# A fused attention-and-MLP block on one core: 128-key V tiles, Q weights ahead of the second token pair, activation tables loaded ahead of use

## The chip, the core and the metric

The kernel runs on one core of a Trainium2 chip. A core has five engines that run their own instruction streams and wait for each other through semaphores: TensorE (PE, matmuls; its weight loads are listed apart as PEld), VectorE (DVE), ScalarE (ACT), GpSimd (POOL) and SyncE (SP, which here only issues DMAs). The metric is the device time of one execution in microseconds (us). Lower is better.

## The reference

Input x has 2048 tokens of width D = 448, all in bf16. Two blocks follow each other.

```
h   = x + A(layernorm(x))            # attention
out = h + B(layernorm(h))            # mixer and MLP

A: qkv = x @ wqkv  (16 heads of 28); each token attends to 8 keys: itself and
   the tokens 2, 4, ... 14 before it; softmax; concat; @ wo
B: h  = gelu(layernorm(x) @ w1)
   h is cut into 4 column groups, shifted along the tokens by +1, -1, +2, -2
   x1 = x + shifted @ w2
   x1 + gelu(layernorm(x1) @ w3) @ w4          # w3: 448 x 1792, w4: 1792 x 448
```

## The kernel before

**Layout.** A partition holds two neighbouring tokens (a = 0, 1: even and odd), and a "pair" m = 0..7 is a block of 128 partitions, 256 tokens. Since a query attends only to tokens of its own parity, even and odd tokens are two separate sequences of 1024. `xin` holds x and later h, `xb` the second residual. `HT` holds the normalised activations transposed: its upper 64 partitions belong to even tokens, the lower 64 to odd ones, in KB = 7 slices of 64 columns of D. A weight matrix is laid out to match: `wload` loads it in two halves, each half of the partitions starting with a different slice (`slot`), and two small transfers fill the slice left over. A matmul over 64 partitions for even tokens and one for odd tokens run in PE at the same time (planner mode "r64").

**Phases.** `phase_LN1(m)` takes statistics on DVE, the inverse root on POOL (`inv_std`: `vtmp`, `rstd`), two normalisations on DVE into `ln`, and a transpose into HT by `ln_to_HT`: on PE with a copy out of PSUM for pairs 0 and 1 (PET = 2), by a DMA transpose on SP's queue for the others. `phase_QK(u, nu)` projects Q (w = 0) and K (w = 1) for 256 x nu tokens per parity, from weights that `wqk_copies` spreads from `wst` (in `h3`) to 32 columns a head (`wqk_p`, in `arena`). `phase_V(t)` makes V for tile t. A tile t of the attention holds 114 queries of each parity in two halves h of NQ = 57, each half with its own 64 keys, which lie on its own 64 partitions. `phase_att(g)` does, for four tiles and one group of four heads, the scores (28x64 matmuls), Exp on ACT, a 0/1 mask on DVE (`msk`), row sums Z by matmuls with a column of ones, Ln and Exp of these on ACT (`lnz`), P·V (64x32 matmuls) and the product with 1/Z on DVE. `phase_WO`, `phase_LN2`, `phase_W1` (with GELU), `phase_W2`, `phase_LN3`, `phase_W3` (with GELU) and `phase_W4` follow. GELU and Exp/Ln need different activation tables, and `emit` puts an ACT_TABLE_LOAD ahead of an operation whose table isn't the loaded one (line 1356).

**Order.** The functions only list operations. `_Sched.schedule` (lines 233 to 377) then orders them, as a list planner with modelled durations: again and again, each engine names the operation that could start first, and among those within SLACK (100 ns) the one of the lowest rank in a list of phase names near the end of `_fast_path`. "flex" operations go to the engine where they would end first. The planner also hands out the 8 PSUM banks. `emit` writes each engine's stream in that order (all operations have line 1360, waits that stand alone line 1358). WARM = 36 matmuls on zeros ("warm") have a low rank.

**End.** `phase_flag` looks for non-finite statistics. Every engine waits for the flag, loads it (line 1398) and branches (1399) over `_general_path`, a full fallback program that doesn't run with these inputs. SP then waits for the outputs (1370), and all engines meet at line 1392.

Of the kernel before, what the change touches and what calls it, by code (L numbers as in the profile page):

```python
# [6 lines left out]
ALU = mybir.AluOpType  # L7
# [8 lines left out]
class _Op:  # L16
    __slots__ = ("idx", "eng", "ins", "kw", "dur", "deps", "users", "sem", "val", "t0", "t1", "clock", "is_dma",
                 "chan", "lat", "bulk", "odeps", "tag", "opts", "table", "prio", "groups", "mode", "xb")

    def __init__(self, idx, eng, ins, dur):  # L20
# [4 lines left out]
        self.is_dma = False; self.bulk = False; self.chan = None; self.lat = 0.0; self.odeps = set()  # L25
# [61 lines left out]
class _Sched:  # L87
# [88 lines left out]
    SWITCH = 300.0  # L176
    LEAD = -300.0
# [4 lines left out]
    def prepare(self):  # L182
        n = len(self.ops)
        for op in self.ops:
            for g in op.groups:
                if g.ops[0] is op:
                    own = set(g.ops)
                    for o in g.ops:
                        if o.eng == "pe":
                            op.odeps |= {d for d in o.deps if d not in own and d.idx < op.idx}  # L190
# [11 lines left out]
    def gated(self, ham, st, work):  # L202
# [3 lines left out]
        while work > 0.0:  # L206
# [7 lines left out]
            ham[1] += step  # L214
# [18 lines left out]
    def schedule(self):  # L233
# [5 lines left out]
        npend = list(self.npend)  # L239
        holder = [None] * 8  # L240
# [46 lines left out]
        table = None  # L287
        mode = None
# [4 lines left out]
        while done < n:  # L293
            best = None
            for e in engs:
                cand = None
                for op in ready[e]:
# [3 lines left out]
                    if cand is not None and st > cand[0] + self.SLACK:  # L301
# [16 lines left out]
                    if e == "act" and op.table is not None and op.table != table:  # L318
                        st = max(st, free[e] + self.TABLE) + self.SWITCH
                    if cand is None or st < cand[0] - self.SLACK or (st < cand[0] + self.SLACK and op.prio < cand[1].prio):  # L320
                        cand = (st, op)
                if cand is not None and (best is None or cand[0] < best[0]):
                    best = cand + (e,)
# [8 lines left out]
            if e == "act" and op.table is not None:  # L332
                if op.table != table:
                    st -= self.SWITCH
                table = op.table
            if e == "pe":
# [3 lines left out]
                dur = self.gated(ham, st, dur)  # L340
# [97 lines left out]
def _fast_path(nc, es, flag, A_x, A_wqkv, A_wo, B_w1, B_w2, B_w3, B_w4, out):  # L438
# [17 lines left out]
    wst = H3[:, 0:KB * 2 * D].rearrange("p (b n) -> p b n", b=KB)  # L456
    wv_s = sb("wv_s", [128, KB, D], BF16)
# [3 lines left out]
    NV = 6  # L461
    WARM = 36
    PET = 2
    NP = 3
    vt = sb("vt", [128, NV, 2, 16, 32], BF16)
    pt = sb("pt", [128, NP, 4, 8 * NQ], BF16)
    lnz = sb("lnz", [128, 2, 2, 8 * NQ], F32)
    lnup = sb("lnup", [128, 1], F32)
    msk = sb("msk", [128, 2, 8 * NQ], BF16)
# [11 lines left out]
    rstd = sb("rstd", [128, 4, 16], F32)  # L481
    vtmp = sb("vtmp", [128, 4, 16], F32)
# [19 lines left out]
    def copy(out_ap, in_ap, n):  # L502
# [3 lines left out]
            "dve": ([("tensor_copy", ka)], (150 + n) / 0.96)}, **ka)  # L506

    last = []

    def dma(chan, out_ap, in_ap, nbytes, dur=450.0, rate=200.0, q="sp", after=(), bulk=False):  # L510
        op = S.macro(q, [("dma_start", dict(out=out_ap, in_=in_ap))], dur, chan=chan, lat=(1200.0, nbytes / rate, 1150.0),
                     after=tuple(after) + tuple(last) if bulk else after, bulk=bulk)
        if bulk:
            last[:] = [op]
        return op
# [19 lines left out]
    def wload(chan, dst, src, qs, after=(), bulk=False, each=False):  # L535
        n = src.shape[1]
        for o in range(2):
            rows = src[64 * o:64 * o + 384, :].rearrange("(i p) n -> p i n", p=128)
            for i in range(3 if each else 1):
                i0, i1 = (i, i + 1) if each else (0, 3)  # L540
                dma(chan + qs[o], dst[:, 2 * i0 + o:2 * i1 + o - 1:2, :], rows[:, i0:i1, :], 128 * n * 2 * (i1 - i0), 500,
                    rate=300.0, q=qs[o], after=after, bulk=bulk)
        for a in range(2):
            dma(chan + qs[a], dst[half[a], 6, :], src[384:448, :] if a == 0 else src[0:64, :], 64 * n * 2, 500, rate=100.0, q=qs[a],
                after=after, bulk=bulk)

    uniq = [0]

    def ch(name):
        uniq[0] += 1  # L550
        return "%s_%d" % (name, uniq[0])

    def load_x(m, q="sp", after=()):
        dma("x%d" % m, xin[:, 2 * m:2 * m + 2, :].rearrange("p a n -> p (a n)"), xrows(A_x, m), 128 * D * 4, rate=333.0, q=q,
            after=after)

    def setup():
        S.tag = "setup"
        load_x(0)
        load_x(1)  # L560
        for w in range(2):
# [872 lines left out]
```

## Time and profile before

| what | value |
|---|---|
| median of 4 runs | 200.5 us (200.3 to 200.95) |
| profiled execution | 201.07 us |
| its span, first to last instruction | 199.3 us |
| PE / PEld / DVE / ACT / POOL busy | 188.6 / 123.3 / 111.1 / 99.2 / 48.3 us |
| instructions | 7192, of these 3279 matmuls and as many weight loads |
| DMA | 18.05 MB, mean 91 GB/s; 312 and 319 GB/s between 5 and 15 us |
| DMA transposes | 22, 3.1 us from issue to landing |
| landings, median | x 5.4 us, Q and K weights 4.4, outputs 1.9 |

A group line gives line, engine, operation, output<-input by the program's names, shape and count, then busy us and mean ns of one, then the idle time just ahead of it and what ended it. "issue" is time in which the engine waited for nothing that the profile shows. PE's matmuls overlap, so the mean ns of one is longer than their spacing; a spacing is found by dividing a group's busy time by its count. In the windows the numbers are the length, the busy time of PE, PEld, DVE, ACT and POOL with the count of instructions, the granted clock, the DMA share and GB/s.

### The profile page before, as it was taken

The numbers are of one execution on the slowest core, as the hardware profiler recorded it, in microseconds if no ns is written. First come the engines' busy times: TensorE is split into PE (matmuls) and PEld (weight loads), VectorE is DVE, ScalarE is ACT, GpSimd is POOL, SyncE is SP. The second block draws the span as 40 slices with busy tenths as digits, with TensorE's granted clock in tenths as the row PEclk, the third lists the DMA queues.
The fourth block names the chain that finished last, engine by engine and source line by source line (L and its number), as shares of the span: only waits on it lengthen the run. The fifth ranks groups of instructions, "written<-read, shape, count | busy, mean of one in ns | idle before, by whom it ended". The sixth has DMA issues, their size and how long they took to land.

```text
span 199.3 us, 7192 instructions
## 1 busy us (share of the span) xinstructions
PE 188.6 (95%) x3279; PEld 123.3 (62%) x3279; DVE 111.1 (56%) x262; ACT 99.2 (50%) x106; POOL 48.3 (24%) x90
## 2 busy tenths in 40 slices
PE   7899999899999999899899999999999999999980
PEld 2377765345455955569767555888875548855540
DVE  6987942653899449999979995100005830012220
ACT  2357689799397998539642400466660004620000
POOL 6313310000045001376330988000000370000000
PEclk9999999999999999999999999999999999999998
DMA  5998692414366333356883617200000160001111
GB/s 171 312 319 145 95 118 63 141 30 129 93 136 121 81 94 102 92 118 96 144 118 104 144 27 167 67 0 3 3 3 0 46 140 3 3 3 44 46 46 56
DMA packets 31515, 18.05 MB, mean 91 GB/s; under 512 B 21368, under 2 KB 31480, under 8 KB 31480
## 3 DMA queue, kind: packets, MB, share of 16 engines
q1 hardware_dynamic: 31480, 17.55, 38.8%
q8 instruction: 26, 0.43, 1.0%
q14 instruction: 9, 0.07, 0.2%
HBM read 10.67 MB, written 1.84 MB: 63 GB/s over the span
## 4 chain that ended last, share of the span: by engine, by line
PE 72%; DVE 11%; ACT 7%; DMA 4%; issue 1%; SPq 1%; POOL 1%
PE ps L1360 72%; DMA h<-in_A_wqkv_dram 3%; ACT QK L1360 2%; DVE xin L1360 2%; DVE QK L1360 2%; ACT lnz L1360 2%; DMA HT<-ln 2%; ACT pt L1360 2%; DVE ln L1360 2%; DVE xb L1360 2%; DVE st L1360 1%; DVE pt L1360 1%; ACT L1356 1%; SPq L1360 1%; POOL rstd L1360 1%
## 5 line engine op out<-in xcount | busy, mean ns | idle before, releaser
L1360 PE MATMUL ps<-HT,w_s 64*128 64x256 bf16 (+1 forms) x1064 | 56.1, 264 | 0.7 <-DMA HT<-ln 0.7
L1360 PEld LDWEIGHTS ps<-HT,w_s 64*128 64x128 bf16 x1064 | 50.5, 94 | 6.5 <-issue 1.1
L1360 DVE TENSOR_TENSOR xb<-ps,xb 128x448 bf16<-128x448 f32 (+1 forms) x24 | 18.6, 773 | 57.0 <-PE ps L1360 57.0
L1360 ACT ACTIVATE arena<-ps 128x1024 bf16<-128x1024 f32 x14 | 14.3, 1024 | 37.8 <-PE ps L1360 37.8
L1360 POOL TENSOR_SCALAR vtmp<-mv 128x2 f32<-128x2 f32 x32 | 6.2, 194 | 111.2 <-DVE mv L1360 109.8
L1360 ACT ACTIVATE QK<-ps 128x1024 bf16<-128x1024 f32 (+2 forms) x24 | 22.5, 952 | 15.3 <-PE ps L1360 15.2
L1360 PE MATMUL ps<-HT,arena 64*128 64x256 bf16 (+1 forms) x336 | 26.4, 305 | 1.0 <-issue 0.9
L1360 POOL TENSOR_TENSOR rstd<-vtmp,mhalf 128x2 f32<-128x2 f32 x32 | 22.1, 691 | 2.7
L1360 PE MATMUL ps<-w_s,arena 128*128 128x448 bf16 x112 | 21.7, 353 | 0.0
L1360 PE MATMUL ps<-w_s,h 128*128 128x448 bf16 x112 | 21.7, 353 | 0.0
L1360 PEld LDWEIGHTS ps<-HT,arena 64*128 64x128 bf16 x336 | 15.6, 94 | 9.6 <-issue 2.2
L1360 DVE BATCH_NORM_STATS2 st<-xin 128x6 f32<-128x448 bf16 x32 | 18.5, 612 | 0.4 <-DMA xin<-in_A_x_dram 0.3
L1360 PEld LDWEIGHTS ps<-w_s,h 128*128 128x128 bf16 x112 | 10.9, 98 | 10.3 <-issue 0.2
L1360 PEld LDWEIGHTS ps<-w_s,arena 128*128 128x128 bf16 x112 | 10.9, 98 | 10.2
L1360 ACT ACTIVATE h<-ps 128x1024 bf16<-128x1024 f32 x14 | 14.2, 1024 | 5.6 <-PE ps L1360 5.5
L1360 POOL TENSOR_TENSOR xb<-xb,xin 128x448 bf16<-128x448 bf16 x16 | 16.6, 1069 | 0.3 <-DVE ln L1360 0.3
L1360 DVE TENSOR_SCALAR ln<-xin,mv,rstd 128x448 bf16<-128x448 bf16 x32 | 14.6, 497 | 2.5 <-POOL rstd L1360 2.5
L1360 ACT ACTIVATE pt<-ps 128x912 bf16<-128x912 f32 x18 | 15.6, 932 | 0.3 <-PE ps L1360 0.2
L1360 DVE TENSOR_TENSOR QK<-ps,lnz 128x456 bf16<-128x456 f32 (+1 forms) x24 | 10.9, 509 | 8.0 <-ACT lnz L1360 4.3
L1360 DVE TENSOR_TENSOR pt<-pt,msk 128x912 bf16<-128x912 bf16 x18 | 11.2, 630 | 6.6 <-ACT pt L1360 5.0
L1360 PE MATMUL ps<-pt 128*128 128x512 bf16 x36 | 11.9, 469 | 1.4 <-DVE HT L1360 1.4
L1360 PE MATMUL ps<-w_s,QK 112*128 112x448 bf16 x64 | 13.0, 353 | 0.0
(53 smaller groups left out, 164.0 us busy)
## 6 DMA issues: line engine op xcount, KB each, us to landing
w_s<-in_B_w_dram SPq DMA_DIRECT2D x19, 224.0 KB, 2.6
xin<-in_A_x_dram SPq DMA_DIRECT2D x8, 224.0 KB, 5.4
out_dram<-xb SPq DMA_DIRECT2D x8, 224.0 KB, 1.9
h<-in_A_wqkv_dram SPq DMA_DIRECT2D x4, 336.0 KB, 4.4
wv_s<-in_A_wqkv_dram SPq DMA_DIRECT2D x2, 336.0 KB, 5.3
w_s<-in_B_w_dram SPq DMA_DIRECT2D x2, 336.0 KB, 3.0
w_s<-in_B_w_dram SPq DMA_DIRECT2D x4, 112.0 KB, 2.6
wo_s<-in_A_wo_dram SPq DMA_DIRECT2D x4, 98.0 KB
```

The costliest lines, as they stand in the source:

```text
L1356: eng.preload_act_table_set(_TABLE_SETS[table])
L1360: inst = getattr(eng, meth)(**kw)
```

## The change

The diff below is cut to its core. What it does, in the order of the code:

- **Planner**: a phase may have a head start (`ahead`, in ns, as `op.bonus`) in the choice among candidates; a PE operation that would run ahead of the modelled instruction fetch is put back; attention matmuls count 0.4 in the modelled clock gate; all ranks are new, and attention is ranked in two parts (attS, attP). When ACT has a modelled gap of 1.2 us or more, the next table is loaded at that gap (`op.load`).
- **Loads**: pair 0 of x comes in two halves, one issued by ACT. Q's weights are issued next, half by ACT, half by SP; then pair 1, then K's weights, pairs 2 and 3. The two small transfers of each `wload` are replaced by copies on ACT or DVE (`cross`).
- **First norm, pairs 0 and 1**: the inverse root by Ln and Exp on ACT. PET is (2, 0, 0) for the three norms, so the same two pairs are transposed by PE, now in two PSUM tiles with two copies. Other norms: the second normalisation of a pair may go to ACT (`normalize2`), for which DVE makes a negated mean.
- **First projection**: one pair at a time (`phase_QKm`), 128 columns a matmul, instead of 256 columns over pairs 0 and 1.
- **V**: 14 matmuls with 128 keys as stationary columns; after the copy into `vt` a DMA brings the rows from 57 on to the lower partitions of `vu`, where the second half's P·V reads.
- **Attention**: a mask may go to POOL.
- **W1** in blocks of 3, 4 and 1 pairs instead of 1, 2, 2, 2, 1. **W4**'s last tile in two halves of 224 columns with their own outputs; the flag's matmul is ordered ahead of these halves. **Fillers**: 20 instead of 36; those from the 13th on come after pair 0's transposes.

```diff
-    NV = 6
-    WARM = 36
-    PET = 2
+    NV = 5
+    WARM = 20
+    PET = (2, 0, 0)
...
+    def cross(dst, src, n):
+        for a in range(2):
+            ka = dict(out=dst[half[a], 6], in_=src[half[1 - a], 5 if a == 0 else 0])
+            S.add("flex", "tensor_copy", 0, opts={
+                "act": ([("activation", dict(ka, func=ACT.Copy))], 170 + n / 1.2),
+                "dve": ([("tensor_copy", ka)], 140 + 0.3 * n)}, **ka)
...
-        for a in range(2):
-            dma(chan + qs[a], dst[half[a], 6, :], src[384:448, :] if a == 0 else src[0:64, :], 64 * n * 2, ...)
+        if dst is not wst_q and dst is not wst_k:
+            S.tag = "cross_" + chan
+            cross(dst, dst, n)
...
-        load_x(0)
-        load_x(1)
-        for w in range(2):
-            wload("wqk%d" % w, wst[:, :, D * w:D * w + D], A_wqkv[:, D * w:D * w + D], ("sp", "sp"))
+        load_x0(0, "sp")
+        load_x0(1, "act")
+        wload("wq", wst_q, A_wqkv[:, 0:D], ("act", "sp"), lat=1900.0)
+        load_x(1)
+        wload("wk", wst_k, A_wqkv[:, D:2 * D], ("sp", "sp"))
         load_x(2)
         load_x(3)
...
+    def inv_std_act(slot, kind, i0, n):
+        act(vtmp[:, slot, i0:i0 + n], mv[:, kind, i0:i0 + n, 1], ACT.Ln, n + 20, bias=epst[:, 0:1])
+        act(rstd[:, slot, i0:i0 + n], vtmp[:, slot, i0:i0 + n], ACT.Exp, n + 20, scale=-0.5)
...
-        if kind == 0 and m < PET:
-            T = tile()
-            pe([("transpose", ...) for b in range(KB)], 7 * 100, "full")
-            copy(HT[...], T(...), 896)
+        if m < PET[kind]:
+            for b0, b1 in ((0, 4), (4, KB)):
+                T = tile()
+                tp = pe([("transpose", ...) for b in range(b0, b1)], (b1 - b0) * 100, "full")
+                if kind == 0 and m == 0:
+                    for o in wops[12:]:
+                        o.odeps.add(tp)
+                copy(HT[...], T(...), 128 * (b1 - b0), 0.5)
             return
...
     def phase_V(t):
+        k0 = 16 + NQ * 2 * t - 7
         for b in range(KB):
-            for h in range(2):
-                for a in range(2):
-                    k0 = 16 + NQ * (2 * t + h) - 7
-                    ins.append(mm(T(lambda p, a=a, h=h: p[half[h], a, 0:D]), HT[half[a], b, k0:k0 + 64], wv_s[half[a], slot(b, a), :], ...))
-        pe(ins, 7 * 190, "r64c64")
+            for a in range(2):
+                ins.append(mm(T(lambda p, a=a: p[:, a, 0:D]), HT[half[a], b, k0:k0 + 128], wv_s[half[a], slot(b, a), :], ...))
+        pe(ins, 14 * 95, "r64")
         copy(vt[:, t % NV, :, :, 0:28], ...)
+        dma("v%d" % t, vu[half[1], t % NV], vt[NQ:NQ + 64, t % NV], 64 * 2048, 500, rate=200.0, lat=1000.0)
...
-                dve("tensor_tensor", (150 + tot) / 0.96, out=pj, in0=pj, in1=msk[...], op=ALU.mult)
+                S.add("flex", "tensor_tensor", 0, opts={
+                    "dve": ([("tensor_tensor", ka)], (150 + tot) / 0.96), "pool": ([("tensor_tensor", ka)], 1950)}, **ka)
...
-                                      vt[half[h], t % NV, a, 4 * c + j, :], pt[...], True, True))
+                                      (vu if h else vt)[half[h], t % NV, a, 4 * c + j, :], pt[...], True, True))
...
+                for n0, n1 in ((0, 224), (224, D)) if (u, k, a) == (3, 1, 1) else ((0, D),):
...
+                    w4s.append(pe(ins, 14 * (n / 2.4 + 2.5), "full", after=w4s if n < D else ()))
...
-        pe([mm(..., fbit[:], ones[:, 0:1], True, True)], 60, "c32")
+        w4s.append(pe([mm(..., fbit[:], ones[:, 0:1], True, True)], 60, "c32"))
...
-    phase_QK(0, 1)
+    phase_QKm(0)
+    phase_QKm(1)
...
-    phase_W1(0, 1)
-    phase_W1(1, 2)
+    phase_W1(0, 3)
...
-    phase_W1(3, 2)
+    phase_W1(3, 4)
-    phase_W1(5, 2)
...
+    for op in S.ops:
+        op.bonus = float(ahead.get(op.tag, 0))
...
-            if op.table is not None and op.table != table:
-                table = op.table
-                eng.preload_act_table_set(_TABLE_SETS[table])
+            if op.load is not None:
+                eng.preload_act_table_set(_TABLE_SETS[op.load])
```

## The prediction

> **What bounds the kernel now.** I read the busy shares first, then the chain of waits, then TensorE (PE) in order of time.
>
> ```profile
> PE 188.6 (95%) x3279; PEld 123.3 (62%) x3279; DVE 111.1 (56%) x262; ACT 99.2 (50%) x106; POOL 48.3 (24%) x90
> ```
>
> PE is the bound, but part of its 188.6 us is filler: matmuls on zeros ("warm"). The groups, shapes kept apart, show the kinds of work (count, then busy us and mean ns):
>
> ```profile
> L1360 PE MATMUL ps<-HT,w_s 64*128 64x256 bf16 x952 | 53.0, 269 | 0.7 <-DMA HT<-ln 0.7
> L1360 PE MATMUL ps<-wv_s,HT 64*64 64x448 bf16 x252 | 12.7, 351 | 0.1
> L1360 PE MATMUL ps<-pt 128*128 128x512 bf16 x36 | 11.9, 469 | 1.4 <-DVE HT L1360 1.4
> L1360 PE MATMUL ps<-HT,w_s 64*128 64x128 bf16 x112 | 3.5, 216 | 0.0
> ```
>
> The 36 fillers hold 11.9 us, so real work is 176.7 us of a span of 199.3: 22.6 us to look for. The chain of waits (start, length, what) shows where they are not:
>
> ```profile
> 9.64 28.40 PE ps L1360 x696
> 38.04 0.87 issue
> ...
> 98.50 95.20 PE ps L1360 x1064
> 193.71 0.02 issue
> 193.73 0.62 DVE xb L1360
> 194.35 0.05 DVE flag L1360
> ```
>
> From 98.5 to 193.7 us PE never stops: nothing but fewer matmul columns shortens that half. Everything else lies before 98.5 or after 193.7. PE in order of time (start, length, and what ended idle time):
>
> ```profile
> 1.45 6.25 PE L1360 MATMUL ps<-pt 128*128 128x512 bf16 x16 [1.45 <-DVE HT L1360]
> ...
> 11.43 6.29 PE L1360 MATMUL ps<-HT,arena 64*128 64x256 bf16 x112
> ...
> 27.14 0.82 PE L1360 MATMUL ps<-pt 128*128 128x512 bf16 x3
> ...
> 34.84 1.04 PE L1360 MATMUL ps<-pt 128*128 128x512 bf16 x4
> ...
> 38.91 0.82 PE L1360 MATMUL ps<-HT,arena 64*128 64x512 bf16 x5 [0.87 <-issue]
> ```
>
> Real projections begin only at 11.43. Between 27 and 36, six runs of fillers (12 matmuls) take, from each one's start to the next group's, 0.75+0.54+0.32+0.32+0.32+0.97 = 3.2 us: PE had nothing ready. The stages, by windows (length, then busy us of each engine):
>
> ```profile
> 26.00:40.00 14.00, 13.13 (x472) 7.41 (x469) 6.84 (x12) 11.75 (x15) 0.00 (x0) 1.00 0.55 106
> 40.00:66.00 26.00, 25.75 (x698) 14.28 (x684) 19.29 (x40) 20.98 (x24) 5.29 (x12) 1.00 0.46 104
> 66.00:98.50 32.50, 30.78 (x766) 22.68 (x763) 27.29 (x61) 24.74 (x27) 10.44 (x18) 1.00 0.49 101
> ```
>
> In 26–40 ScalarE (ACT, 11.75 of 14) starves PE; in 66–98.5 VectorE (DVE, 27.29 of 32.5) does, for 1.7 us; POOL has room in both. Last, the end: DVE writes the flag at 194.4, and every engine loads it and branches over the fallback program.
>
> ```profile
> L1399 PEldq COMPARE_BRANCH x1: 3934/3934/3934, 195.0 to 195.0; - x1
> ```
>
> PE's branch takes 3.93 us, the other engines' under 0.1; PE's drain is last, at 199.0. SyncE (SP) is through by 196.6, so the last output's landing (2.0 us) is hidden.
>
> **The change part by part**, against the profiled execution (201.07 us, span 199.3). The median of the runs is 200.5, 0.57 below it; I subtract that at the end.
>
> *Start.* Q's weight load passes the second token pair in the queue, is split over the SP and ACT queues, and its two small cross-half transfers become on-chip copies. Before, Q's weights landed at 8.32 behind two x loads and four weight transfers, 1.26 MB; afterwards 0.92 MB stand ahead. At the window's 290–320 GB/s that is about 1.1 us less: about 7.2. The copies (DVE 0.42 each) put the first Q matmul near 8.1. The first token pair's HT will be there: its x half-tiles go out at 0.8 on two queues, two statistics (0.6 each), the inverse root now on ACT in two short operations (the nearest, a one-column Exp, took 0.20) instead of POOL's 0.27+0.73, two normalisations (0.45 each), transposes 0.56 and a copy. But the second pair and K's weights now stand behind Q: with landings of 5.4 us for x, and K at 10.87 before, both are ready near 11.3, as now. So only the first quarter of the projection (m=0, Q) leaves the path: 6.9/4 = 1.7 us. Bounds: 0 (all arrives late) to −3.2 (the whole block moves). I take **−1.7**.
>
> *PE work.* V: 28 matmuls 64*64 become 14 of 64*128. Four tiles now fill 56.66 to 62.08, 1.36 each. The 256-column form costs 53.0/952 = 55.7 ns, the 512-column form 3.13 us/28 = 111.8 (45.64 to 48.77), so 448 columns cost 97.7 and 14 make 1.37. V saves no PE time, only 252 matmul and load instructions. The first projection in 128-column pieces: 224 × 31 (3.5 us/112) = 6.9 against 6.2: +0.7. W1 in blocks of 3, 4 and 1 pairs: 56 × (83.7 + 111.8 + 31) = 12.7 against 168 × 55.7 + 3.5 = 12.9: −0.2. Sum **+0.5** (−0.3 to +0.8). "Two DMA transposes in place of TensorE ones" I do not find: PET is 2 before and (2,0,0) after, so pairs 0 and 1 of the first norm stay on PE, in two PSUM tiles each; 0.
>
> *Fillers, 27–36.* 36 become 20: twelve at the start, eight after the first transposes, none need stand here. Their 3.2 us come back only as far as real work is there. The masks (18 × 0.63) may go to POOL, idle here, and V_3, late at 31.45, ranks early; but ACT, the one that is full, gains only half-normalisations and cross copies. I take two thirds, **−2.2** (0 to −3.2).
>
> *The 0.87 "issue" idle at 38.0*: PE's own sequencer; PE has some 250 fewer matmul-and-load pieces net and 32 fewer of fillers. **−0.4** (0 to −0.9).
>
> *66–98.5.* PE idles 1.7 us here behind DVE. Masks to POOL, every second normalisation (0.45) to ACT, against one-column negated means (0.1 to 0.2 each) added. The table loads (1.28 at 66.8, 71.0 and 90.0) move into ACT gaps; PE ran on through all three, so they are worth nothing by themselves, and if a gap is misjudged one costs 1.3. **−1.2** (+1.5 to −1.7).
>
> *V by DMA.* Keys 57 to 120 of each tile go through SP to the other half of the partitions before P·V. The hop is about an issue (0.4) and a landing (2.0, as the last output): 2.4. Before, P·V began at 34.23, 0.3 after V_3's copy, and at 63.70, 0.6 after V_7's: unless V moves earlier, each is exposed. On SP the waiting transfer holds back the DMA transposes and loads queued behind it, on which QK_2 and W1 wait. Issues balance: 12 cross loads less, 9 hops, one x half and 3 outputs more. I take **+0.4** (0 to +4.8), since V's inputs are there 10 us earlier.
>
> *End.* The flag's matmul now precedes the last W4 groups, so PE loads it right after its last matmul (193.6 instead of 194.4), perhaps earlier; the branch stays. The halved last tile only shortens what is hidden. **−0.9** (0 to −1.5).
>
> *Clock.* In the start row above fillers come 0.43 us apart until 6.55, then faster: 5.3 us of dense work were needed. Twelve make 5.1 us; if the rise is missed, the first Q quarter doubles to 3.5 and still ends at 11.6, 0.3 late: nothing taken. [...]
>
> Sum: −1.7 +0.5 −2.2 −0.4 −1.2 +0.4 −0.9 = −5.5; 201.07 − 5.5 − 0.57 = **195.0 us**.
>
> **The rivals.**
>
> *Starvation moves.* PE starts earlier, runs out of work earlier and meets the same x loads, transposes and exponentials. For it: 26–40 is full on ACT. Against it: POOL is empty there. Only the end (−0.9) and 0.5 of the start remain: 199.1.
>
> *Masks on POOL (slower).* POOL's 128x448 sum takes 1.07 us, so a 912-column mask up to 2.14 against DVE's 0.63: 1.5 us more between Exp and the row sums. If PE waits for it, each costs 1.5; with four of 18 exposed the gain is gone, with five (+7.5 − 5.5) the time is 202.5. For it: the attention stage waits on just this link (DVE pt behind ACT pt, 5.0 us over 5 waits). Against it: the planner prices POOL and sends a mask there only when DVE ends later. [...]
>
> *It does not do what it says.* The transposes stay, V saves nothing on PE; had the other terms no effect either, 200.5.
>
> **How the numbers follow.** Forecast (190.5 to 197.5) 0.62; starvation moves 0.16; no effect 0.04; masks or V hop late 0.18. All gains at their best give −10.8, or 189.7; all costs without a gain +7.1. The range 190.5 to 201.0 leaves out about 0.04 below and 0.15 above. A difference under 0.3% (199.9 to 201.1) cannot be told from none: faster 0.78, same 0.04, slower 0.18.
>
> **What would show it.** First 64x128 matmul on arena near 8.1; no filler after 15 us; no V time saved on PE; under 1.7 us PE idle and DVE below 27 us in the old 66–98.5 work; PE's flag load within 0.2 us of its last matmul, the 3.9 us branch still there; a PE stretch of about 95 us unbroken before the end. POOL masks that PE's row sums wait for, or "DMA vt" ahead of P·V, would make it wrong.

## The result: 0.4 per cent faster, not three

The changed kernel takes 200.27 us (median of 52 runs; 198.19 to 203.51) beside 200.59 for the kernel before. The ratio of times is 0.9962, interval 0.9951 to 0.9973: about 0.8 us less, where 5.5 less was forecast. Medians and ranges are over all runs; the ratios leave out runs over 1.5% above the fastest of the same kernel (here 15 of 54, 13 of them with a mean granted clock of 0.991 or less), and by the medians of all runs the gain is only 0.3 us. The profiled execution shown here lies near the lower end, 198.47 us with a span of 196.8; a second one (`a_rep` below) took 201.19 with 199.3.

The page of the changed kernel, busy shares; then the groups that the forecast priced, shapes kept apart (busy us, mean ns | idle time before them):

```profile
PE 184.1 (94%) x3151; PEld 117.5 (60%) x3151; DVE 119.7 (61%) x294; ACT 105.5 (54%) x120; POOL 50.0 (25%) x89
```

```profile
L1476 PE MATMUL ps<-wv_s,HT 64*128 64x448 bf16 x126 | 13.1, 350 | 1.1 <-DVE wv_s L1476 0.6 <-DMA HT<-ln 0.5
...
L1476 PE MATMUL ps<-HT,arena 64*128 64x128 bf16 x224 | 6.9, 216 | 0.0
...
L1476 PE MATMUL ps<-pt 128*128 128x512 bf16 x20 | 6.5, 468 | 2.4 <-DVE pt L1476 1.5 <-ACT HT L1476 0.9
```

DVE is 8.6 us busier than before; V costs PE what it cost. PE in order of time (start, length, and what ended idle time):

```profile
8.76 2.52 PE L1476 MATMUL ps<-HT,arena 64*128 64x128 bf16 x84
...
13.28 1.50 PE L1476 MATMUL ps<-wv_s,HT 64*128 64x448 bf16 x14 [0.61 <-DVE wv_s L1476]
...
19.71 1.50 PE L1476 MATMUL ps<-wv_s,HT 64*128 64x448 bf16 x14 [0.48 <-DMA HT<-ln]
...
26.16 1.25 PE L1476 MATMUL ps<-pt 128*128 128x512 bf16 x5
...
77.93 4.71 PE L1476 MATMUL ps<-wo_s,QK 128*128 128x448 bf16 x24 [0.71 <-DVE QK L1476]
...
84.43 1.69 PE L1476 MATMUL ps<-wo_s,QK 128*128 128x448 bf16 x8 [1.27 <-DVE xin L1476]
...
105.47 7.78 PE L1476 MATMUL ps<-HT,w_s 64*128 64x512 bf16 x112 [0.68 <-DMA HT<-ln]
```

The first projection begins 2.67 us earlier and only one run of fillers stands after 26 us, but there are new waits. The 0.71 stands ahead of WO_3 (the output projection, WO, for pair 3), the 1.27 ahead of WO_5; before, four projections followed each other without one, and the one wait for DVE stood ahead of some scores:

```profile
80.83 0.44 PE L1360 MATMUL ps<-QK 28*64 28x57 bf16 x32 [0.50 <-DVE QK L1360]
81.37 6.23 PE L1360 MATMUL ps<-wo_s,QK 128*128 128x448 bf16 x32
```

At the start it was not Q's weights that came last. ACT spreads them from 6.32 on and only then copies the first pair's transposes out of PSUM, until 8.55, though PE had finished these transposes at 6.88:

```profile
6.32 1.36 ACT L1476 ACTIVATE arena<-h 64x448 bf16<-64x448 bf16 x2 [1.02 <-DMA h<-in_A_wqkv_dram]
7.59 0.96 ACT L1476 ACTIVATE HT<-ps 128x512 bf16<-128x512 bf16 x2
```

The stages (length, then busy us of PE, PEld, DVE, ACT, POOL, granted clock, DMA share, GB/s):

```profile
26.00:40.00 14.00, 13.97 (x417) 8.35 (x403) 10.72 (x18) 13.74 (x16) 0.51 (x1) 1.00 0.62 135
40.00:66.00 26.00, 25.78 (x598) 13.30 (x594) 23.01 (x51) 20.29 (x24) 5.54 (x12) 1.00 0.55 132
66.00:98.50 32.50, 29.62 (x751) 20.14 (x750) 28.96 (x71) 24.45 (x27) 13.04 (x21) 1.00 0.48 115
98.50:140.00 41.50, 40.72 (x444) 25.41 (x444) 27.13 (x71) 16.36 (x18) 21.07 (x32) 1.00 0.30 64
```

26 to 40 is mended (13.97 of 14). From 66 to 98.5 PE is busy 29.62 instead of 30.78 and DVE 28.96 instead of 27.29 (in `a_rep`, where the same work lies some 2.5 us later, 27.02; a fixed window is a rough measure). The chain of waits, one stretch of PE from 98.5 to the end before, now runs over the other engines as late as 138:

```profile
77.24 1.17 DVE QK L1476 x2
78.44 1.83 DVE w_s L1476
80.30 1.15 DVE st L1476 x2
...
82.03 0.70 POOL rstd L1476
...
83.38 2.01 DVE xin L1476 x2
...
102.53 2.90 DMA HT<-ln
105.47 10.93 PE ps L1476 x128
...
138.65 53.72 PE ps L1476 x574
```

**A ledger of lost time.** From the trace's start times I took, for every shape of matmul, the mean distance to the next one (gaps of 0.3 us and more left out, the same means for all kernels), and subtracted from a time t the sum over the real matmuls begun by t. What is left is the time PE has lost by then to waiting, fillers and a halved clock (us; entries are good to about 0.2):

| lost by t = | 26 | 40 | 60 | 66 | 98 | 192 |
|---|---|---|---|---|---|---|
| before | 10.4 | 15.6 | 16.7 | 16.9 | 19.3 | 19.4 |
| changed, first profile | 9.4 | 11.4 | 12.3 | 13.0 | 17.3 | 18.0 |
| changed, `a_rep` | 9.8 | 12.0 | 12.9 | 15.4 | 19.6 | 20.6 |
| searched order, `r_1` | 9.6 | 11.4 | 12.7 | 13.4 | 17.4 | 17.9 |
| W1 in parts, `d_w1` | 9.4 | 11.4 | 12.3 | 13.3 | 24.0 | 24.1 |

By 60 us the change leads by 4.4 and 3.8 us. From 60 to 98 the kernel before loses 2.6 and the changed one 5.0 and 6.7; from there to 192 it loses 0.7 and 1.0 more, the kernel before 0.1. That is where the gain goes. PE's waits of over 0.15 us between 60 and 98 tell the same: they sum to 0.8 before, 2.6 in the first profile, 4.7 in `a_rep` and 2.3 in `r_1`. The first profile adds 0.71 ahead of WO_3 and 1.27 ahead of WO_5; `a_rep` has both again (0.77 and 1.27) and 2.11 more ahead of W1.

### The profile page after: what moved, and what is told of

Read it like the earlier page. It is cut to its first block, busy times and chain, and to the rows that moved or that the text cites. A ratio compares the mean times of both kernels' runs of the same rounds, so it can differ in the third digit from the quotient of the medians.

```text
span 196.8 us, 6998 instructions
## 1 busy us (share of the span) xinstructions
PE 184.1 (94%) x3151; PEld 117.5 (60%) x3151; DVE 119.7 (61%) x294; ACT 105.5 (54%) x120; POOL 50.0 (25%) x89
## 4 chain that ended last, share of the span: by engine, by line
PE 54%; DVE 25%; DMA 8%; POOL 7%; ACT 2%; issue 1%
PE ps L1476 54%; DVE st L1476 8%; DMA HT<-ln 7%; DVE ln L1476 4%; POOL rstd L1476 4%; DVE xb L1476 3%; DVE xin L1476 3%; POOL xb L1476 2%; DVE mv L1476 1%; DVE nmr L1476 1%; DVE QK L1476 1%; DVE arena L1476 1%; DMA xin<-in_A_x_dram 1%; DVE w_s L1476 1%; ACT lnz L1476 1%
## 5 line engine op out<-in xcount | busy, mean ns | idle before, releaser
L1476 PE MATMUL ps<-HT,w_s 64*128 64x256 bf16 (+3 forms) x952 | 56.1, 275 | 1.1 <-DMA HT<-ln 0.9
L1476 DVE TENSOR_TENSOR xb<-ps,xb 128x448 bf16<-128x448 f32 (+2 forms) x25 | 18.6, 747 | 57.2 <-PE ps L1476 57.2
L1476 PEld LDWEIGHTS ps<-HT,w_s 64*128 64x128 bf16 x952 | 44.7, 94 | 12.3 <-DMA HT<-ln 1.8
L1476 PE MATMUL ps<-HT,arena 64*128 64x128 bf16 (+2 forms) x448 | 26.9, 270 | 0.0
L1476 ACT ACTIVATE arena<-ps 128x1024 bf16<-128x1024 f32 x14 | 14.3, 1024 | 16.9 <-PE ps L1476 16.9
L1476 PE MATMUL ps<-w_s,arena 128*128 128x448 bf16 (+1 forms) x126 | 21.7, 332 | 0.0
L1476 PEld LDWEIGHTS ps<-HT,arena 64*128 64x128 bf16 x448 | 17.0, 94 | 6.8 <-ACT HT L1476 0.4
L1476 ACT ACTIVATE QK<-ps 128x1024 bf16<-128x1024 f32 (+2 forms) x19 | 18.3, 981 | 3.4 <-PE ps L1476 3.1
L1476 PE MATMUL ps<-wo_s,QK 128*128 128x448 bf16 x64 | 13.0, 353 | 2.0 <-DVE xin L1476 1.3
L1476 PE MATMUL ps<-wv_s,HT 64*128 64x448 bf16 x126 | 13.1, 350 | 1.1 <-DVE wv_s L1476 0.6
L1476 DVE TENSOR_SCALAR ln<-xin,mv,rstd 128x448 bf16<-128x448 bf16 x25 | 11.8, 496 | 0.6 <-ACT rstd L1476 0.6
```

The costliest lines, as they stand in the source:

```text
L1476: inst = getattr(eng, meth)(**kw)
```

## The experiments

Where "the order is kept", the planner of the changed kernel runs as it is, and its finished order is edited. Each kernel was timed in five rounds beside the kernel before; ratios are to that. The diffs are cut: `...` marks what is left out, and the words behind `#` are added here.

**`a_rep`: the changed kernel again.**

> The changed kernel, unaltered. Its runs so far spread from 198.2 to 203.5 us where the kernel before stays within 199.9 to 202.0. [...] DMA theory: the spread is in landings; the clock is 1.00 throughout and a projection or a DMA transpose starts later than in the first profile. Median 200.0 to 200.6.

200.94 us (198.78 to 204.61), ratio 0.9949 (0.9919 to 0.9979). The profile, 2.5 us longer than the first, has one great difference: PE stands ahead of the W1 block of pairs 0 to 2 (W1_0). First the first profile, then `a_rep`:

```profile
63.66 4.83 PE L1476 MATMUL ps<-HT,w_s 64*128 64x384 bf16 x56
```

```profile
63.88 0.39 PE L1476 MATMUL ps<-pt,ones 64*32 64x456 bf16 x8
66.38 4.72 PE L1476 MATMUL ps<-HT,w_s 64*128 64x384 bf16 x56 [2.11 <-ACT lnz L1476]
```

The clock stands at 1.00 in both, so this profile speaks for the DMA theory, transfers. The named releaser only ended at about that time: in the first profile this block began at 63.66, as the reading of `lnz` from PSUM began. What the block does read is the transposes of three pairs, and SyncE's queue (SPq) shows them back to back, one of them issuing for 2.36 us where the other two take 1.30, the last issued at 62.24 and 4.1 us (the median of the three) from landing:

```profile
56.59 1.29 SPq L1476 DMA_DIRECT2D vu<-vt  x2
58.49 5.05 SPq L1476 DMA_TRANSPOSE HT<-ln  x3
```

In the first profile the three took 4.13 us and PE waited 0.1. Before, W1 began with pairs 1 and 2, and pair 0's transpose, issued at 63.15, was first read at 68.18.

**`a_mask`: the one mask on POOL back on DVE**, order kept.

```diff
+    for o in list(order["pool"]):
+        if o.opts and o.tag == "attS_2_0":
+            _move(S, order, o, "dve")
```

> The changed kernel with its order frozen, but the one mask that was sent to POOL (last attention group) done by DVE in its place. Sharing theory: in the first profile that mask (1.92 us) ran beside a 64x896 DVE copy that took 1.82 us instead of 0.39 and PE stood still for 1.27 us behind DVE; with the mask on DVE (0.63) the copy falls back to 0.4, PE's wait ahead of the fifth output projection nearly goes, and the time falls by 1.0 to 1.5 us. If that idle stretch is also what lets the clock drop in some runs, the runs above 201.5 us become rarer and the median falls by up to 2. Rival (the copy was slow for another reason, or PE waits for something else there): no change within 0.3.

200.03 us (198.44 to 206.02), ratio 0.9945 (0.9919 to 0.9972): no difference. Beside POOL's mask (78.10 to 80.02) the DVE copy of W3's cross half had taken 1.82 us, without it 0.39:

```profile
78.44 1.82 DVE L1476 COPY w_s<-w_s 64x896 bf16<-64x896 bf16 x1
```

```profile
79.82 0.39 DVE L1509 COPY w_s<-w_s 64x896 bf16<-64x896 bf16 x1
...
83.72 0.21 DVE L1509 TENSOR_SCALAR nmr<-mv,rstd 128x1 f32<-128x1 f32 x1 [0.58 <-POOL rstd L1509]
83.85 0.50 DVE L1509 TENSOR_SCALAR ln<-xb,mv,rstd 128x448 bf16<-128x448 bf16 x1
84.26 2.08 DVE L1509 SCALAR_TENSOR_TENSOR xin<-ps,xin 128x896 bf16<-128x896 f32 x2
```

But PE still waited 1.06 at WO_5: the mask now takes DVE's time, and DVE stands 0.58 for POOL's inverse root with the residual adds, for which PE waits, behind that in its order. The wait changed its cause, and hardly its length.

**`a_dense`: four fillers directly behind the first transposes**, order kept.

```diff
+    w[11].ins = w[11].ins * 2
+    w[12].ins = w[12].ins * 2
+    _drop(S, order, w[13:15])
```

> The changed kernel with its order frozen; the four fillers that follow the first transposes stand directly behind them (two in each of the first two PSUM tiles) instead of two of them waiting 0.92 us for a PSUM tile; the count is the same. [...] Rival (the spread comes from a later idle stretch or from DMA): the same spread and median within 0.3.

199.70 us (198.97 to 202.89), ratio 0.9957 (0.9917 to 0.9996): nothing to be told apart. When the clock rises matters little: at 4.4 us in the first profile and 7.2 in `a_rep`, with the first projection at 8.76 and 8.90. Nor did the clock stay up: five of the eight runs have a mean of 0.986 to 0.988, and this profile shows PE's clock halved from 80.14 to 83.55 us, in the middle of the work (24 matmuls of WO take 6.40 us there, 4.71 in the first profile). Behind that stretch PE doesn't wait at WO_5 (85.97), though DVE has all its work: slowed, PE comes late enough by itself. So a missing wait at WO_5 says nothing in a profile with a halved clock just ahead of it.

**`b_tail`: the new end alone, in the kernel before.**

```diff
+                for n0, n1 in ((0, 224), (224, D)) if (u, k, a) == (3, 1, 1) else ((0, D),):
...
-        pe([mm(..., fbit[:], ones[:, 0:1], True, True)], 60, "c32")
+        w4s.append(pe([mm(..., fbit[:], ones[:, 0:1], True, True)], 60, "c32"))
```

> The kernel before with the end alone changed: the flag's matmul ordered ahead of the last W4 groups, the last tile in two halves of 224 columns, outputs of the last 512 tokens one tile at a time. My forecast's step for the end: PE loads the flag right behind its last matmul, the 3.9 us branch stays, 0.9 us less (0 to 1.5), so 199.7. Rival: the outputs take over as the last thing, under 0.3 less. All in all the changed kernel's end, from PE's last matmul to the end of the span, measured 4.45 us against 5.6.

Slower: 202.03 us (6 runs; five from 201.66 to 202.88, one of 321.19 with a mean clock of 0.564), ratio 1.0071 (1.0045 to 1.0097). PE's flag load came at 191.5, before its last matmul, as meant. But ACT, which sends the last output, did so 1.8 us late:

```profile
193.40 0.39 DVE L1369 TENSOR_TENSOR xb<-ps,xb 128x224 bf16<-128x224 f32 x1 [0.95 <-PE ps L1369]
...
195.59 0.37 ACTq L1369 DMA_DIRECT2D out_dram<-xb  x1
```

ACT's semaphore event stands at 193.83, an instruction transfer (queue q14) at 195.03, the issue at 195.59. In the changed kernel no such transfer lies there, and the issue follows the add at once (192.39, then 192.81). By this one trace, then, the end brings its microsecond only where no fetch of code falls into it; that the fetch made ACT late is read from its place in time and was not tested.

**`c_v`: V as before the change**, order kept.

```diff
...
+    for o, ins in _ALT.items():   # V in 28 matmuls of 64x64; P.V reads vt for both halves
+        o.ins = ins
+    _drop(S, order, [o for o in order["sp"] if o.tag[:2] == "V_"])
```

> The changed kernel with its order of work kept, but V computed as before (28 matmuls of 64x64 per tile straight into both halves of the partitions) and the nine transfers from vt to vu gone; P.V reads vt for both halves. Theory (the hop crowds the transfer queue in front of the three transposes that the 384-column W1 block needs): PE's wait ahead of W1_0, 0.0, 0.4, 0.5 and 2.0 us so far in four profiles of the same stage, is under 0.4; the transposes take 1.2 to 1.4 us of issue each and none 1.5 to 2.4; PE's V time stays within 0.3 us of 13.1; median 0.5 to 1.5 us below the changed kernel's (ratio to before 0.988 to 0.993). Rival (the hop is hidden, and the wait comes from asking for three transposes at once): W1_0 still waits 0.4 to 2 us and the ratio stays at 0.994 to 0.997.

199.31 us (198.87 to 200.18), ratio 0.9941 (0.9919 to 0.9964): the rival, or little more. Without any hop the transposes still took 5.02 us for three, one of them 2.34:

```profile
59.10 5.02 SPq L1532 DMA_TRANSPOSE HT<-ln  x3
```

and PE stood 1.02 ahead of W1_0. So the hop is not what stretches a transpose; what does stays open (before, the first of three took 1.79). Its nine runs lie closer together than the others.

**`c_fix`: five waits edited at once**, order kept.

```diff
...                               # mask on DVE; unread negated means dropped; fillers as in a_dense
+    order["sp"] = [o for o in sp[:k + 1] if o not in hop] + hop + [o for o in sp[k + 1:] if o not in hop]
...
+    order["dve"] = dv[:k] + add + [o for o in dv[k:] if o not in add]    # WO adds ahead of LN3_1
```

> The changed kernel with its order kept but for five small edits: the one mask that went to POOL back on DVE, the 18 negated means that nobody reads dropped, four fillers directly behind the first transposes, two V hops behind the three transposes at 58 to 62 us instead of ahead of them, and two residual adds of WO ahead of the LN3 normalisations that wait for POOL. Theory (the expected gain sits in a few waits that the written order brings: W1_0 on a transpose, WO_5 on DVE's residual add): the wait at WO_5 (1.3 us) is gone, W1_0 waits under 0.5, PE's waits sum to about 5 instead of 7.6 to 9.4, and the median falls 1.5 to 2.5 below the changed kernel's (ratio 0.983 to 0.988). Rival (each wait removed only uncovers the next, DVE and ACT being near full where they stand): PE's waits keep their sum within 1 us and the ratio stays at 0.992 to 0.997.

200.32 us, ratio 0.9943 (0.9912 to 0.9974): the rival. W1_0 still waits 1.04, with two hops moved behind its transposes. No wait stands at WO_5, but the clock is halved just ahead (79.04 to 82.46; the 24 matmuls of WO there take 6.33 us instead of 4.71), so that shows nothing. With the normalisations put behind the adds, PE now waits for the transposes of W3_0:

```profile
89.95 1.26 PE L1543 MATMUL ps<-HT,w_s 64*128 64x256 bf16 x20 [1.40 <-DMA HT<-ln]
```

**`c_late`: x pairs 1 and 2 ahead of the second half of Q's weights**, order kept.

```diff
+    x = [o for o in sp if o.chan in ("x1", "x2")]
+    order["sp"] = sp[:1] + x + [o for o in sp[1:] if o not in x]
```

> The changed kernel with its order kept, except that the loads of the second and third token pair go out ahead of the second half of Q's weights on the SP queue, as the second pair's did before. Q's weights land about 1 to 1.5 us later and the first projection begins at 9.8 to 10.3 instead of 8.8. Theory of the forecast (the start lies on the path to the end, each us there is a us of the whole): 0.8 to 1.5 us slower than the changed kernel, ratio to before 0.998 to 1.004. Rival (an earlier start is given back at the next waits, V_0 on its weights, V_2 on a transpose): those two waits (1.1 us) shrink by what the start lost and the ratio stays at 0.993 to 0.997.

201.46 us, ratio 1.0025 (0.9993 to 1.0057), 1.3 us above the changed kernel. That is the theory's figure, but not its way: the first projection began at 8.86, hardly later, and V_0 0.5 later than in `a_rep`. Q's weights did come later: the last of the copies that spread them ended at 8.33, instead of 7.68 in the first profile. But ACT's copies of the first pair's transposes, done at 8.65, were still the last thing that the projection needed. The profile, of a longer run (203.31), has 1.93 at W1_0 and a halved clock from 67.19 to 70.60. So the run doesn't price a start that really moves.

**`c_tail`: the last tile whole and the outputs in pairs**, in the changed kernel.

```diff
-                for n0, n1 in ((0, 224), (224, D)) if (u, k, a) == (3, 1, 1) else ((0, D),): ...
-                        dma("out%d_%d_%d" % (m, a, n0), ..., q="sp" if n0 == 0 else "act")
+            dma("out%d" % m, xrows(out, m), xb[:, 2 * m:2 * m + 2, :].rearrange("p a n -> p (a n)"), 128 * D * 4)
```

> The changed kernel with the end of before: the flag's matmul after the last output tile, whole last tile, outputs in pairs on the SP queue. Theory (the end was worth what the forecast said, about 0.9, as the 4.45 us from PE's last matmul to the end against 5.58 before show): 0.7 to 1.3 us slower than the changed kernel, ratio to before 0.998 to 1.003, and the tail is 5.4 to 5.8 us. Rival (the tail depends on where the blocks of code lie that the engines fetch, as the 1.8 us late ACT transfer in the kernel before with the new end suggests): the tail is within 0.4 us of 4.45, or longer than 6.5.

200.01 us, ratio 0.9977 (0.9948 to 1.0005). The flag's matmul kept its early place (PE's flag load at 190.1), so this undoes only the halved tile and the outputs: from PE's last matmul (193.6) to the end 4.3 us, as with them. They are worth nothing that can be measured. That leaves the flag's place for the end's gain (the planner put its matmul at 104.63 us in the changed kernel, at 193.62 before); no run moved the flag back alone.

**`d_w1`: half of the W1 block in parts**, so that 1.5 us of work stands ahead of the third transpose; order kept.

```diff
...
+        first, rest = slice(0, 256), slice(256, 384)
+        x.ins = [(m, dict(kw, out=cut(kw["out"], first), rhs=cut(kw["rhs"], first), stop=False)) for m, kw in o.ins]
+        o.ins = [(m, dict(kw, out=cut(kw["out"], rest), rhs=cut(kw["rhs"], rest), start=False)) for m, kw in o.ins]
```

> The changed kernel with its order kept; only the first two of the four tiles of the 384-column W1 block are computed in two parts, first the 256 columns of pairs 0 and 1 of both tiles, then the 128 columns of pair 2, so that 1.5 us of work stands ahead of the first use of the third transpose (28 more matmuls, about 0.15 us of PE time). Theory (the block of three pairs, one of the change's parts, makes PE wait for three transposes at once where before it needed them one after the other): PE's wait at W1_0, 0.0 to 2.1 us and about 1.0 in the middle of eight profiles, falls below 0.4, and the median falls 0.5 to 1.0 (ratio to before 0.991 to 0.994). Rival (what is won there is lost at WO_5, where DVE is the bound): the wait at WO_5 grows from 1.3 to about 2 and the ratio stays at 0.994 to 0.997.

Slower: 203.42 us (201.10 to 205.31), ratio 1.0059 (1.0023 to 1.0096). The wait at W1_0 fell to 0.18, and by 66 us no more was lost than in the first profile, give or take 0.3. Then:

```profile
72.30 0.31 PE L1543 MATMUL ps<-QK 28*64 28x57 bf16 x6 [2.11 <-issue]
72.54 3.17 PE L1543 MATMUL ps<-w_s,QK 112*128 112x448 bf16 x8
```

```profile
66.00:98.50 32.50, 29.33 (x654) 17.37 (x650) 23.21 (x51) 20.13 (x23) 10.24 (x15) 0.74 0.39 89
```

PE waits 2.11 us for nothing that the profile shows, the clock halves at 71.64 and stays so until 88.71 (three slices of the page running have 0.5), and eight matmuls take 3.17 instead of 1.69. From 66 to 98 it loses 10.7 us, the first profile of the changed kernel 4.3, for 28 more matmuls with their weight loads. An instruction transfer (queue q8) stands at 69.92, but the first profile has one at 69.78 too, and no wait; so what the 2.11 us are stays open. The halved clock is the larger part of the loss: 17.07 us at half pace can cost up to 8.5 of the 10.7.

**`d_dve`: DVE relieved**, W3's cross halves loaded from DRAM as before the change, unread negated means dropped; order kept.

```diff
...
+        o.ins = [("dma_start", dict(out=_DST[o], in_=src))]      # the four cross_w3 copies
...
+    _drop(S, order, [o for o in nm if o not in live])            # 18 negated means
```

> The changed kernel with its order kept, DVE relieved: the four copies of W3's cross halves (3.0 us of DVE, one of them 1.8 beside POOL's mask) are loads from DRAM again as before the change, and the 18 negated means that nobody reads (3.7 us) are dropped. The POOL mask stays. Theory (DVE's added work makes PE wait in the stage from 66 to 90 us): the wait at WO_5 (1.3 us, the same in six of seven profiles) falls below 0.5, W3_0 begins 1 us earlier after the same W1_0, and the median falls 0.7 to 1.3 (ratio 0.989 to 0.993). Rival (DVE waits for POOL's inverse roots there, and the adds that PE needs stand behind them in DVE's order): WO_5 still waits 1.0 or more and the ratio stays at 0.994 to 0.997.

198.90 us (196.15 to 199.48, 6 runs), ratio 0.9870 (0.9813 to 0.9926): the theory, and faster than the changed kernel. The medians of all six runs give 0.9915; the lowest one pulls the ratio down. No wait stands at WO_5, but this profile has 3.4 us of halved clock among the WO tiles (6.40 instead of 4.71), which hides the wait in `a_dense` too:

```profile
78.53 6.40 PE L1545 MATMUL ps<-wo_s,QK 128*128 128x448 bf16 x24 [0.66 <-DVE QK L1545]
84.85 0.39 PE L1545 MATMUL ps<-pt,ones 64*32 64x456 bf16 x8
85.17 1.69 PE L1545 MATMUL ps<-wo_s,QK 128*128 128x448 bf16 x8
```

**`e_w3` and `c_nmr`: the two halves of that.** Only the copies become loads; only the negated means go.

> The changed kernel with its order kept; only the four copies of W3's cross halves on DVE (3.0 us, one of 1.8 beside POOL's mask) become loads from DRAM again. The unread negated means stay. Theory A (the long copy, made long by the mask on POOL beside it, is what holds DVE up ahead of WO_5): the wait at WO_5 falls from 1.3 to below 0.5 and the ratio to before is 0.987 to 0.992, most of what both edits together brought (0.987). Theory B (it was the sum of DVE's work): WO_5 waits about 0.8 and the ratio is 0.991 to 0.995.

> The changed kernel with its order kept; only the 18 negated means that nobody reads are dropped (3.7 us of DVE, 0.2 each, 0.1 where they follow one another closely). Theory A (they lie in DVE's own waits for POOL's inverse root and cost next to nothing): WO_5 still waits 1.0 to 1.3 and the ratio is 0.993 to 0.997. Theory B (the sum of DVE's work): WO_5 waits 0.5 to 0.9 and the ratio is 0.990 to 0.993.

`e_w3`: 199.91 us, ratio 0.9934 (0.9903 to 0.9964). `c_nmr`: 200.13 us, ratio 0.9954 (0.9923 to 0.9984). Ahead of WO_5, first `e_w3`, then `c_nmr`:

```profile
84.92 1.69 PE L1541 MATMUL ps<-wo_s,QK 128*128 128x448 bf16 x8 [0.32 <-DVE xin L1541]
```

```profile
85.86 1.69 PE L1526 MATMUL ps<-wo_s,QK 128*128 128x448 bf16 x8 [1.28 <-DVE xin L1526]
```

Both profiles have a clock of 1.00 there. The wait is the copies' (theory A of both); in time they bring 0.3% over the changed kernel, the range of theory B, with intervals that overlap. The 3.7 us of unread means cost nothing that can be measured. The two halves together bring less than `d_dve` did; why is open, and its few runs may be all there is to it.

**`d_all`: `d_w1`, `d_dve` and the mask on DVE together.**

> Both edits together (the W1 block in parts; W3's cross halves as loads and no unread negated means), and the one mask back on DVE. Theory (two waits, W1_0 and WO_5, hold what the forecast expected of this stage): PE's waits between 60 and 98 us fall from 3.0 to 4.8 to under 2, and the median falls 1.5 to 2.3 (ratio 0.985 to 0.989). Rival (the stage is bound by the chain norm, transpose, W1, W2, norm, transpose, W3, whatever PE does): the waits reappear ahead of W3_0 and the ratio is 0.992 or more.

204.02 us, ratio 1.0052 (1.0011 to 1.0094). Neither theory: the stall on issue is there again (2.29 at 72.37) with halved clock from 72.32 and again from 82.56, 3.41 us each (eight matmuls take 3.17 at 72.61, 1.69 at 76.40). W1_0 doesn't wait (0.03), and what DVE's relief is worth can't be seen beside the stall.

**`r_1`: the same operations in another order.** The planner's priorities were searched anew with dearer transposes and loads; the POOL mask and the unread means are out.

```diff
-        trs.append(S.add("sp", "dma_start_transpose", 1222.0, chan=ch("tr"), lat=(450.0, 1250.0, 1200.0),
+        trs.append(S.add("sp", "dma_start_transpose", 1282.0, chan=ch("tr"), lat=(450.0, 1250.0, 1800.0),
...
-                     after=tuple(after) + tuple(last) if chan[0] in "xw" else after, bulk=bulk)
+        op = S.macro(..., lat=(lat, nbytes / rate, 1400.0 if chan[0] in "xw" else 1150.0), ...
...
-        "setup LN1_0 wcopy0 QKm_0_0 QKm_1_0 ...
+        "attS_0_2 LN2_1 QK_2_0_2 W2_0 W2_7 ...
```

> The changed kernel's operations, all of them (but the unread negated means and the POOL mask), in another order: the kernel's own planner run again with priorities searched anew, with transposes 0.66 us and weight and token loads 0.25 us dearer, so that no step is planned to the moment at which its transpose lands. Theory (the operations of the change are worth what the forecast said for the start, the fillers and the end; the written order gives it back at waits that its prices did not hold): median 197.0 to 198.5 (ratio 0.983 to 0.990), and the runs lie within 3 us of each other. Rival (the waits come with the operations, not with their order): 199 or more (ratio above 0.992), with new waits of 1 us or more between 60 and 98 us.

198.55 us (198.12 to 199.04), ratio 0.9898 (0.9864 to 0.9932): the theory, at its upper end. It beats the kernel before by 1.0% and the changed one by 0.6%, and its six runs lie within 0.9 us. One transpose is now issued at 53.80, the other two at 59.03, and W1_0 doesn't wait:

```profile
64.11 4.72 PE L1532 MATMUL ps<-HT,w_s 64*128 64x384 bf16 x56
```

Nor does it in the profiles of `s_1` and `s_2`, which keep this order; in the eleven profiles of the changed kernel and its edits that leave the block whole it waits 0.1 to 2.1, in the middle 1.0. By 66 us `r_1` has lost 13.4; the largest wait left between 60 and 98 is 1.27 at 79.08 on an exponential of ACT. Its profile (198.12) is hardly faster than the changed kernel's best run (198.19): what the order brings is mostly that the longer runs are gone.

**`s_1`: `r_1` with W3's cross halves loaded. `s_2`: `r_1` with V as before.**

> The searched order (median 198.55, ratio 0.9898) with its order kept, and W3's cross halves loaded from DRAM instead of copied on DVE. Theory (both causes stand side by side: the order's tight places and DVE's copies): the wait for DVE's residual add at 84.5 us (0.4) is gone, 0.5 to 1.2 us less than the searched order, 197.4 to 198.1 (ratio 0.984 to 0.988). Rival (without the POOL mask a copy takes 0.39 us and the searched order has room for it): 198.3 to 198.8.

> The searched order with its order kept, and V computed as before the change (28 matmuls of 64x64 straight into both halves, no transfer from vt to vu). It gives V's part of the change its price where no other wait hides it. Theory of the forecast (V by DMA costs 0.4, PE's time for V is the same): 0.0 to 0.6 us less than the searched order, 197.9 to 198.6. Rival (V in 128-key tiles saves what it was meant to, 126 matmuls and weight loads): 0.3 to 1.0 more, 198.9 to 199.6.

`s_1`: 199.30 us (197.53 to 200.69), ratio 0.9899 (0.9864 to 0.9935), no gain over `r_1`: the rival; with no mask on POOL and this order the copies cost nothing that can be measured. `s_2`: 199.27 us, ratio 0.9931 (0.9907 to 0.9955), 0.3% above `r_1`, the rival's side, though the intervals touch. V's new form is no loss that can be measured once its hop has room.

## Why the prediction was wrong, step by step

- **Start (−1.7).** Q's weights were on the chip near 6.3, sooner than the 7.2 forecast, yet the first projection began at 8.76, not near 8.1: "HT will be there" was wrong, ACT's copy into HT came last (8.55). That is still 2.67 us earlier than before, but the ledger has only 0.6 to 1.0 of it left at 26 us. Two waits of V stand in between (0.61 on a cross copy of its weights, 0.48 on a transpose): cross copies were priced for Q alone.
- **Fillers (−2.2) and issue (−0.4).** From 26 to 40 us the loss fell from 5.2 to 2.0 and 2.2: −3.2 and −3.0. The mechanism was right and somewhat under-sized (−2.6 forecast for the two terms). That PE's sequencer was behind the 0.87 of issue no run shows; the profile names no cause for it. With the start it makes −3.6 to −4.2 where −4.3 was forecast.
- **PE work (+0.5).** The sum of the ledger's mean slots went from 174.3 to 174.1 (−0.1 before rounding; no better than a few tenths). The 128-column form goes out every 28.9 ns in the mean, the 256-column form every 55.1, so the first projection grew by 224 × 28.9 − 112 × 55.1 = 0.3 us rather than 0.7.
- **66–98.5 (−1.2): the step that failed.** From 60 to 98 us the loss grew by 2.4 (first profile) and 4.1 (`a_rep`) over the kernel before, where 1.2 less was forecast. There was less to win than the term took: of the 1.7 us that it put to DVE, one wait of 0.50 ended on DVE (80.83), one of 0.27 on ACT and one of 0.69 on a transpose (98.50). And two terms were missing. The first is W3's cross copies, which the sum never counted: beside the one mask on POOL a copy was stretched from 0.39 to 1.82 us, and PE waited 1.27 at WO_5. The rival on masks saw POOL's cost, but in PE waiting for the mask, not in a slowed DVE copy. Taking the copies off DVE shortens that wait to 0.32 (`e_w3`), taking the mask off POOL hardly does (1.06). The second is W1 in blocks of 3, 4 and 1, priced by its columns (−0.2), not by what it waits for: 0.1 to 2.1 us at W1_0 in the order as written, none in the searched one. (The 0.7 at 105 us is not new; before, it stood at 98.50.) How full DVE is was the wrong thing to look at: `c_nmr` took 3.7 us off DVE and gained nothing that can be measured, and `r_1` has DVE at 29.07 in the same window and is faster. The 0.71 ahead of WO_3 was tested by no run.
- **V by DMA (+0.4).** No price was seen: `c_v` is 0.2% below the changed kernel, `s_2` 0.3% above its own, both within the intervals.
- **End (−0.9).** From PE's last matmul to the end 4.45 us instead of 5.58: −1.1. The halved tile and the outputs are worth nothing in it (`c_tail`), so by elimination it is the flag's place.
- **Clock (nothing taken).** The danger was seen at the start, where it hardly moved the first projection (8.76 and 8.90), and not in the body (below). The 5.3 us of dense work that the prediction read from one trace are no fixed need: fillers began at 1.45 in all, and the clock rose at 6.80 before, at 4.45 in the first profile and at 7.21 in `a_rep`.

For the first profile, then: −4.4 by 60 us, +2.4 by 98, +0.6 after, −0.1 of work, −1.1 at the end make −2.6; measured against the profiled execution before, 198.47 − 201.07 = −2.6. For `a_rep`: −3.8 +4.1 +0.9 −0.1 −1.1 = 0.0; measured +0.1.

"No effect" (200.5) came nearest to the median, by luck: the early gains are there, and are lost again. "Starvation moves" (199.1) comes nearest in kind, but for another reason: not ACT between 26 and 40, which was mended, but a DVE copy and the transposes after 60. `r_1` shows that a part of this was order: nearly the same operations (the POOL mask and the unread means, worth nothing each by itself, are out) reach 198.55, without the wait at W1_0. That falls short of 195.0 too: between 60 and 98 it still loses 4.7, against 5.0 and 6.7 in the changed kernel and 2.6 before, with 1.27 and 0.41 of it ahead of two WO tiles. Whether any order of these operations avoids that stays open.

## What to carry to other kernels

A lead won early is worth only what the later stages can take. Look there first for each wait and what ended it; the busy share of the next engine (here DVE, 28 of 32 us) didn't tell which work cost anything. Price everything that the change adds to that engine, and ask what runs beside it. An order made by a planner is as good as its most optimistic price; give transfers some slack and repeat the profile, since one trace can miss a wait of 2 us. Price a coarser block by what it must wait for, not only by its columns. And see whether the clock was halved in a stretch before reading from it that a wait is gone.

## What the runs showed of the hardware

- PE's granted clock fell to 0.5 in the middle of the work, in stretches of 3.41 us (`a_dense`, `c_late`, `d_all` twice; 3.42 in `c_fix`) and of 17.07, five times as long, in `d_w1`. In the changed kernel 19 of 66 runs have a mean clock of 0.989 or less, with a median of 202.1 us, and the 31 at 0.995 or more have 200.0; in the kernel before no run of 107 fell below 0.991. So the longer runs mostly go with a lower clock. What is cause and what effect isn't shown: five of `r_1`'s six runs have 0.985 to 0.987 and take 198.5 to 199.0, hardly more than the one at 1.0 (198.12). Ahead of the drop in `a_dense` PE's idle pieces were 0.77, 0.56 and 0.66 us, among small attention matmuls.
- Beside a two-input operation on POOL (the mask, 1.92 us) a DVE copy of 64x896 took 1.82 us; with that mask on DVE (`a_mask`) it took 0.39. The copy ended 0.25 us after the POOL operation (80.27 and 80.02). What the two engines share there isn't shown. The mask itself took three times DVE's 0.63.
- In `b_tail` 1.8 us passed on ACT between a semaphore event and the instruction behind it (193.83 to 195.59), with an instruction transfer in between (195.03).
- In the changed kernel PE reaches its flag load and branch ahead of its last matmuls' end (190.6 against 192.4), so that the branch over the fallback program, 4.85 us there, 4.06 in `a_rep`, 3.58 in `a_dense` and 5.27 in `a_mask`, is partly hidden.
